# Keeping the tiled matmul pieces together by priority instead of by fences, with two score blocks in one bank

## The chip, the cores and the metric

The kernel runs on one core of a Trainium2 chip. The core has five engines that run their own instruction queues side by side: TensorE (PE, the matmuls; PEld is its weight load), VectorE (DVE), ScalarE (ACT), GpSimd (POOL) and SyncE (SP, which only issues DMA transfers here). Each engine takes its instructions strictly in the order in which they were put into its queue; semaphores make one engine wait for another. The metric is the time of one execution in microseconds (us), measured on the device; lower is better.

## The reference

The program is a causal attention with a decay, followed by a gated MLP. Cut to what matters:

```python
# q, k, v: 8 batches x 8 heads x 576 tokens x 64;  f: 8 x 8 x 576
scores = q @ k.T / 8
decay  = cumsum(log f)[:, None] - cumsum(log f)[None, :]
scores = where(causal, -1e9, scores + decay)
attn   = exp(scores - max) / (sum + 1e-9)
x      = concat_heads(attn @ v)                 # 8 x 576 x 512
h = relu(x @ w_in); u, v = halves of h          # 512 columns each
v_n = (v - mean) / sqrt(var + 1e-6)
v_s = w_spatial @ v_n + b_spatial               # over the 576 tokens
out = (u * v_s) @ w_out
```

## The kernel before

**Work units.** Attention goes by pairs of heads: 32 pairs P, four to a batch. One pair's two heads (h = 0, 1) lie in the two halves of the 128 partitions: head 0 in rows 0 to 63, head 1 in rows 64 to 127. The MLP ("moe" in the code) goes by batches, eight of them. The outer loop at the end of the kernel writes attention of batch b+1 and the MLP of batch b interleaved, at a pace set by the numbers that the generators yield. The order so written is the priority order; the tile framework's scheduler then decides, for each engine, in which order the instructions really stand in its queue. It may take a later instruction first when an earlier one is not yet ready in its own timeline.

**Attention of one pair.** `scores(P)` makes, for each of the first four 128-row blocks i of queries and each head, one matmul of 64 contraction rows (L257): block i sees 128·(i+1) keys, so its output has 128, 256, 384 or 512 columns. The output tile is `sc` (PSUM pool `s`, four banks). `lowest` (L243, DVE) adds the decay `dk` and writes the result into `tt`, one tile for each head, `tt0` and `tt1`, which exist once only; ACT takes the exponential in place (L267); DVE makes the reciprocal sums `sm` (L270, L271); POOL multiplies each block by them (L275). `transposes(P, h)` turns the blocks of `tt` with TensorE (L321, into `tp`, PSUM pool `t`, two banks), and the results are copied into `e` by ACT and DVE in turn (L313). The last 64 queries of both heads are done together in `scores_tail` (matmul at L201 into `sc`, then tile `tl`) and `transposes_tail` (L332). `attend` (L350) multiplies `e` with the raw V: 14 matmuls into two `sc` tiles, x0 (queries 0 to 255) and x1 (the rest); the two heads write the two halves of the output partitions. `prep(P)` loads `qk_t` (two buffers), `dk` and `dt` (one buffer each) through SP and masks `dk` and `dt` on POOL (L216, L218, L222).

**Tiled pieces.** The matmuls of `scores` use 64 of the array's 128 rows each, those of `attend` 64 of its 128 columns, so those of head 0 and head 1 can run at the same time when they stand next to each other. The kernel calls such a group a piece. There are three pieces for each pair: score blocks 0 and 1, score blocks 2 and 3, and `attend`. `in_one_piece` and `queued` put fences around them: every matmul and transpose that is written before a piece must stand in TensorE's queue before it, everything written after it must stand behind it, and the matmuls inside it are chained one behind the other.

**MLP of one batch.** First the v half: five groups of matmuls into `ps` (PSUM pool `ps_m`, two banks) and the normalization (L424 to L437). Then the u half (L448), then for two token ranges the spatial product (L466 to L471), the gate `u` (L474, DVE), its split into `gh` (L477, ACT) and `gl` (L478, POOL), and `w_out_tile` (L494), two at a time, which multiplies four `gh`/`gl` pairs j = 0 to 3 with `w_out`. The matmuls that use `gl` of j = 3 cannot start before POOL has made it.

**Startup.** At the start weights are loaded and split into high and low parts by DVE, ACT and POOL (`load64`, L114 to L128), beside the attention of batch 0 alone.

## Time and profile before

| | |
|---|---|
| runs of the kernel before | 878.43, 881.36, 887.39 us (median 881.36) |
| the profiled execution's own time | 876.43 us |
| its span, first to last instruction | 874.7 us |
| granted TensorE clock, mean | 0.965 |
| DVE busy, share of the span | 444.2 us, 51% |
| ACT busy | 415.0 us, 47% |
| POOL busy | 383.5 us, 44% |

The profile is one execution. A row with "busy" gives the time in which an engine had at least one instruction under way. Idle time before an instruction is put down to the engine whose semaphore came last. Matmuls overlap in the array, so the duration of one is longer than the distance from its start to the next one's start; the distance between starts is what a matmul costs in a full stream.

### The profile page before, as it was taken

What the parts mean: (1) busy time and instruction counts of PE and PEld (TensorE: products, weight loads), DVE (VectorE), ACT (ScalarE), POOL (GpSimd) and SP (SyncE); (2) the same over time, 40 slices, a digit from 0 to 9 for tenths busy, and PEclk for the clock granted to TensorE, in tenths of its full rate; (3) what the DMA queues carried; (4) which work ended last, traced back from release to release, by engine and by line L of the source; (5) the groups of instructions that cost most, each with busy time, mean ns of one, the idle gap of its engine ahead of it and who ended that gap; (6) DMA issues with size and microseconds to landing.
All of it is one profiled execution on the core that took longest, in us unless ns stands there. A gap on an engine that the chain in (4) does not pass through costs nothing.

```text
span 874.7 us, 14557 instructions
## 1 busy us (share of the span) xinstructions
PE 789.7 (90%) x4933; PEld 610.6 (70%) x4934; DVE 444.2 (51%) x1482; ACT 415.0 (47%) x1092; POOL 383.5 (44%) x703
## 2 busy tenths in 40 slices
PE   5677889988998989988999889989899889999997
PEld 2344557876687867866688767867678766787896
DVE  6865856334654537445564336445463345643131
ACT  3565655434554435544564336544554345643231
POOL 4875675443544236334453336343354434432141
PEclk8677889999999999999999999999999999999999
DMA  6545531233232233233321243322322333101001
GB/s 232 169 140 144 164 95 64 85 112 112 88 88 73 67 97 88 88 112 85 99 73 62 83 123 89 88 85 64 102 65 85 112 106 90 50 26 40 25 1 61
DMA packets 35213, 79.44 MB, mean 91 GB/s; under 512 B 4161, under 2 KB 8257, under 8 KB 35138
## 3 DMA queue, kind: packets, MB, share of 16 engines
q1 hardware_dynamic: 34818, 77.98, 29.7%
q8 instruction: 39, 0.64, 0.3%
q10 hardware_dynamic: 320, 0.52, 0.2%
q14 instruction: 36, 0.29, 0.1%
HBM read 68.73 MB, written 9.75 MB: 90 GB/s over the span
## 4 chain that ended last, share of the span: by engine, by line
PE 52%; POOL 16%; ACT 7%; issue 6%; DVE 3%; DMA 3%; POOLq 0%; SPq 0%; ACTq 0%; DVEq 0%
PE ps L201 29%; PE sc L350 7%; POOL tt L275 7%; PE sc L257 5%; PE tp L321 5%; PE sc L201 3%; POOL vnl L433 3%; ACT tt L267 3%; DMA dt<-rows_d 3%; PE tp L201 2%; POOL gl L478 2%; ACT e L313 2%; POOL dk L218 1%; POOL dk L216 1%; PE tp L332 1%
## 5 line engine op out<-in xcount | busy, mean ns | idle before, releaser
L275 POOL TENSOR_SCALAR tt<-tt,sm 128x128 f32<-128x128 f32 (+3 forms) x256 | 134.6, 545 | 149.3 <-DVE sm L271 121.4
L267 ACT ACTIVATE tt<-tt,nm 128x128 f32<-128x128 f32 (+3 forms) x256 | 141.3, 554 | 56.2 <-DVE nm L243 55.5
L321 PE MATMUL tp<-ident,tt 128*128 128x128 f32 x640 | 104.5, 290 | 35.6 <-ACT e L313 20.4
L478 POOL TENSOR_TENSOR gl<-u,gh 128x256 fp32r<-128x256 f32 (+1 forms) x64 | 51.5, 804 | 178.5 <-ACT gh L477 178.4
L321 PEld LDWEIGHTS tp<-ident,tt 128*128 128x128 f32 x640 | 77.4, 146 | 55.6 <-ACT e L313 25.6
L313 DVE COPY e<-tp 128x128 f32<-128x128 f32 (+2 forms) x160 | 66.9, 420 | 90.0 <-PE tp L321 73.6
L257 PE MATMUL sc<-qk_t 64*128 64x384 f32 (+3 forms) x512 | 97.4, 492 | 9.6 <-DVE nm L243 9.6
L313 ACT COPY e<-tp 128x256 f32<-128x256 f32 (+2 forms) x160 | 75.6, 478 | 61.6 <-PE tp L321 49.8
L350 PE MATMUL sc<-e,vraw 128*64 128x320 f32 (+4 forms) x896 | 96.1, 365 | 2.7 <-DVE nm L243 1.6
L350 PEld LDWEIGHTS sc<-e,vraw 128*64 128x64 f32 x896 | 60.2, 139 | 43.0 <-issue 4.5
L201 PE MATMUL ps<-xh,winh 128*128 128x256 f32 (+1 forms) x232 | 74.5, 321 | 0.5 <-ACT vx L424 0.5
L201 PE MATMUL ps<-sph,vnh 128*128 128x256 f32 (+1 forms) x240 | 74.7, 311 | 0.0
L201 PE MATMUL ps<-woh,gl 128*128 128x512 f32 x112 | 45.3, 406 | 29.2 <-POOL gl L478 29.2
L201 PE MATMUL ps<-spl,vnh 128*128 128x256 f32 (+1 forms) x240 | 71.5, 298 | 0.0
L201 PE MATMUL ps<-sph,vnl 128*128 128x256 f32 (+1 forms) x240 | 71.4, 297 | 0.0
L201 PE MATMUL ps<-xl,winh 128*128 128x256 f32 (+1 forms) x232 | 68.5, 295 | 0.0
L201 PE MATMUL ps<-xh,winl 128*128 128x256 f32 (+1 forms) x232 | 68.5, 295 | 0.0
L257 PEld LDWEIGHTS sc<-qk_t 64*128 64x128 f32 x512 | 44.6, 202 | 34.0 <-DVE nm L243 16.8
L356 DVE TENSOR_TENSOR xl<-sc,xh 128x256 fp32r<-128x256 f32 x64 | 29.1, 454 | 75.7 <-ACT xh L355 75.5
L243 DVE CUSTOM_DVE_ANT_1 tt<-sc,dk 128x512 f32<-128x512 f32 (+1 forms) x128 | 66.5, 553 | 1.0 <-PE sc L257 0.9
L243 DVE CUSTOM_DVE_ANT_0 tt<-sc,dk 128x384 f32<-128x384 f32 (+1 forms) x128 | 49.4, 421 | 34.6 <-PE sc L257 32.4
L201 PE MATMUL ps<-winh,xh 128*128 128x512 f32 x148 | 63.4, 429 | 0.0
(165 smaller groups left out, 1680.3 us busy)
## 6 DMA issues: line engine op xcount, KB each, us to landing
dk<-rows_d SPq DMA_DIRECT2D x64, 320.0 KB, 4.0
qk_t<-in_dram SPq DMA_DIRECT2D x32, 608.0 KB, 4.6
vraw<-in_dram SPq DMA_DIRECT2D x32, 320.0 KB, 2.9
dt<-rows_d SPq DMA_DIRECT2D x64, 144.0 KB, 4.4
out_dram<-o SPq DMA_DIRECT2D x32, 256.0 KB, 2.0
w<-in_dram SPq DMA_DIRECT2D x8, 512.0 KB, 5.0
w<-in_dram SPq DMA_DIRECT2D x8, 256.0 KB, 3.3
wraw<-in_dram SPq DMA_DIRECT2D x4, 288.0 KB, 7.3
```

Source lines behind the costliest of these rows:

```text
L201: queued(T.matmul(o, l, r, start=st, stop=sp))
L216: G.affine_select(out=two, in_=two, compare_op=ALU.is_ge, fill=-8.0 * BIG, base=0, pattern=[[0, 2], [-1, 128]], channel_multiplier=1)
L243: V.tensor_tensor_reduce(out=out, in0=ps, in1=dec, scale=-0.125, scalar=3.0e38, op0=ALU.add, op1=ALU.min, accum_out=acc_)
L257: made.append(T.matmul(sc[i, h][:, 0:n], qk_t[p, n - 128:n], qk_t[p, 640:640 + n], start=True, stop=True))
L267: last["exp", P, h, i] = A.activation(t, t, AF.Exp, bias=nm[h][:, i:i + 1], scale=-1.0, accum_out=sm[h][:, i:i + 1])
L275: G.tensor_scalar(out=t, in0=t, scalar1=sm[h][:, i:i + 1], scalar2=1.0, op0=ALU.mult, op1=ALU.mult)
L313: (V.tensor_copy if nev[0] % 2 == 1 else A.copy)(out, ps)
L321: queued(T.transpose(out=tp[:, (i - c) * 128:(i - c + 1) * 128], in_=tt[h][:, TOFF[i] + 128 * c:TOFF[i] + 128 * c + 128], identity=ident))
L350: made.append(T.matmul(x[64 * h:64 * h + 64, q0 - s0:q1 - s0], vt[:, c, h, :], e[:, h, e0 + q0:e0 + q1], start=c == 0, stop=c == end))
L356: V.tensor_tensor(out=xl[:, s0:s0 + n], in0=ps[:, 0:n], in1=f32(xh[:, s0:s0 + n]), op=ALU.subtract)
L433: G.tensor_tensor(out=tlo, in0=x, in1=f32(th[:]), op=ALU.subtract)
L478: G.tensor_tensor(out=gl[j][:, 0:nt], in0=g, in1=f32(gh[j][:, 0:nt]), op=ALU.subtract)
```

## The change

Three things change.

1. The fences go. Plain matmuls and transposes are issued without any edge. A piece is now given as a list of jobs: its first matmul is issued like any other instruction; each further one is issued at the highest priority, with an edge that puts it behind the one before it in TensorE's queue. Nothing keeps other matmuls out from between two matmuls of a piece when the second one is not ready in the scheduler's timeline.
2. The two score pieces are cut in another way: blocks 0, 1 and 2 in one, block 3 alone in the other, and within a piece from the largest block down. Blocks 0 and 1 of a head share a bank (columns 0 to 127 and 128 to 383), so the first piece needs four `sc` tiles, as before, and the second two where it needed four. The pace numbers are unchanged as formulas.
3. `transposes_tail` does blocks 4 and 3 before 0, 1 and 2, and `attend` lists x1 before x0.

```diff
-    def queued(i):
-        if fence:
-            behind(i, fence[0])
-        open_.append(i)
-        return i
-
-    def in_one_piece(made):
-        for n, i in enumerate(made):
-            for j in open_ if n == 0 else (made[n - 1],):
-                behind(i, j)
-        open_.clear()
-        fence[:] = [made[-1]]
+    def in_one_piece(jobs):
+        was = None
+        for n, job in enumerate(jobs):
+            if was is None:
+                was = job()
+            else:
+                with tc.high_priority():
+                    i = job()
+                behind(i, was)
+                was = i
 
     def mm(o, l, r, st, sp):
-        queued(T.matmul(o, l, r, start=st, stop=sp))
+        T.matmul(o, l, r, start=st, stop=sp)
...
-        for piece in ((0, 1), (2, 3)):
-            made, sc = [], {}
+        for piece in ((0, 1, 2), (3,)):
+            at = {}
             for i in piece:
                 for h in range(2):
-                    sc[i, h] = PS['s'].tile([128, 512], F32, name="sc")
-                    p, n = slice(64 * h, 64 * h + 64), 128 * (i + 1)
-                    made.append(T.matmul(sc[i, h][:, 0:n], qk_t[p, n - 128:n], qk_t[p, 640:640 + n],
-                                         start=True, stop=True))
-            in_one_piece(made)
+                    if i == 1:
+                        at[i, h] = at[0, h][0], 128
+                    else:
+                        at[i, h] = PS['s'].tile([128, 512], F32, name="sc"), 0
+
+            def product(i, h):
+                ps, c = at[i, h]
+                p, n = slice(64 * h, 64 * h + 64), 128 * (i + 1)
+                return lambda: T.matmul(ps[:, c:c + n], qk_t[p, n - 128:n], qk_t[p, 640:640 + n],
+                                        start=True, stop=True)
+
+            in_one_piece([product(i, h) for i in reversed(piece) for h in range(2)])
...
-        for cs, off, step in (((0, 1, 2), 512, 512), ((4, 3), 576, 640)):
+        for cs, off, step in (((4, 3), 576, 640), ((0, 1, 2), 512, 512)):
...
-            for x, s0, q0, q1, end in ((x0, 0, 128 * c, 256, 1), (x1, 256, lo, S, NB)):
-                for h in range(2) if c <= end else ():
-                    made.append(T.matmul(x[64 * h:64 * h + 64, q0 - s0:q1 - s0], vt[:, c, h, :],
-                                         e[:, h, e0 + q0:e0 + q1], start=c == 0, stop=c == end))
-        in_one_piece(made)
+            for x, s0, q0, q1, end in ((x1, 256, max(256, 128 * c), S, NB), (x0, 0, 128 * c, 256, 1)):
+                jobs += [product(x, s0, q0, q1, c, h, end) for h in range(2) if c <= end]
+        in_one_piece(jobs)
```

The softmax rows after a score piece follow the new order of blocks (largest first within a piece). In the new code `lowest` stands at L238, the score matmuls at L258, plain matmuls at L196, the transposes at L325 and L336, `attend` at L352, the POOL scaling at L279 and `gl` at L484.

What this does to the queues is shown at three places. First TensorE, at the scores of the tenth pair (P = 9), beside the v half of an MLP. In the names `sc` are score banks, `ps` the MLP's banks, `tp` the transposes' banks, `tt_82` and `tt_83` the tiles of head 0 and head 1. Before:

```order
L321 MATMUL tp<-ident,tt_82 128x128 x3
L321 MATMUL tp<-ident,tt_83 128x128 x10
L257 MATMUL sc<-qk_t 128x128 x2
L257 MATMUL sc<-qk_t 128x256 x2
L201 MATMUL ps<-winh,xh 128x512
L201 MATMUL ps<-winl,xh 128x512
L201 MATMUL ps<-winh,xl 128x512
L201 MATMUL ps<-winh,xh 128x512
L201 MATMUL ps<-winl,xh 128x512
L201 MATMUL ps<-winh,xl 128x512
L257 MATMUL sc<-qk_t 128x384 x2
L257 MATMUL sc<-qk_t 128x512 x2
```

Both pieces stand whole, behind all transposes of the pair before. Now, the first piece at the same pair:

```order
L258 MATMUL sc<-qk_t 128x384 x2
L258 MATMUL sc<-qk_t 128x256
L196 MATMUL ps<-winh,xl 128x512
L196 MATMUL ps<-winh,xh 128x512
L196 MATMUL ps<-winl,xh 128x512
L258 MATMUL sc<-qk_t 128x256
L258 MATMUL sc<-qk_t 128x128 x2
L325 MATMUL tp<-ident,tt_82 128x128
L325 MATMUL tp<-ident,tt_83 128x128 x4
```

The piece is cut between the 256-column matmul of head 0 and that of head 1, and it stands ahead of the last transpose of head 0 and all of head 1. Now, the second piece at this pair:

```order
L258 MATMUL sc<-qk_t 128x512
L196 MATMUL ps<-winh,xh 128x512
L196 MATMUL ps<-winl,xh 128x512
L196 MATMUL ps<-winh,xl 128x512
L196 MATMUL ps<-winh,xh 128x512
L196 MATMUL ps<-winl,xh 128x512
L258 MATMUL sc<-qk_t 128x512
L325 MATMUL tp<-ident,tt_83 128x128 x5
```

Five MLP matmuls stand between the two heads' 512-column matmuls. Over the whole program TensorE's queue has 92 unbroken runs of tiled matmuls before and 127 now. For the pairs P = 5 to 31, which lie where TensorE is nearly always busy, 14 pieces are cut between the 256-column matmuls of the two heads, 11 between the 512-column ones, and 5 more between two blocks (behind both 384-column matmuls); three times a score piece now joins directly to an `attend`.

Second POOL, at the last gate product of a `w_out` group (j = 3, the row with `gl`) while the scores of P = 8 are scaled (`tt0`, `tt1`) and the next pair's `dk` is masked. Before:

```order
L275 TENSOR_SCALAR tt0_82<-tt0_82,sm_2119 128x256
L275 TENSOR_SCALAR tt0_82<-tt0_82,sm_2119 128x384
L275 TENSOR_SCALAR tt0_82<-tt0_82,sm_2119 128x512
L216 AFFINE_SELECT dk_2268<-dk_2268 128x2x128
L218 AFFINE_SELECT dk_2268<-dk_2268 128x256
L275 TENSOR_SCALAR tt1_83<-tt1_83,sm_2120 128x128
L275 TENSOR_SCALAR tt1_83<-tt1_83,sm_2120 128x256
L275 TENSOR_SCALAR tt1_83<-tt1_83,sm_2120 128x384
L275 TENSOR_SCALAR tt1_83<-tt1_83,sm_2120 128x512
L216 AFFINE_SELECT dk_2269<-dk_2269 128x2x128
L218 AFFINE_SELECT dk_2269<-dk_2269 128x256
L478 TENSOR_TENSOR gl_2158<-u_1597,gh_2157 128x320
```

Now:

```order
L484 TENSOR_TENSOR gl_2045<-u_1467,gh_2044 128x320
L484 TENSOR_TENSOR gl_2089<-u_1530,gh_2088 128x320
L279 TENSOR_SCALAR tt0_82<-tt0_82,sm_2103 128x128
L279 TENSOR_SCALAR tt0_82<-tt0_82,sm_2103 128x256
L279 TENSOR_SCALAR tt0_82<-tt0_82,sm_2103 128x384
L279 TENSOR_SCALAR tt0_82<-tt0_82,sm_2103 128x512
L211 AFFINE_SELECT dk_2250<-dk_2250 128x2x128
L213 AFFINE_SELECT dk_2250<-dk_2250 128x256
L484 TENSOR_TENSOR gl_2128<-u_1583,gh_2127 128x320
L279 TENSOR_SCALAR tt1_83<-tt1_83,sm_2104 128x128
L279 TENSOR_SCALAR tt1_83<-tt1_83,sm_2104 128x256
L279 TENSOR_SCALAR tt1_83<-tt1_83,sm_2104 128x384
```

The last `gl` of the group stands ahead of head 1's four scalings and two masks instead of behind them. This holds at all such groups in which a pair's scaling falls between the third and the fourth `gl`.

Third TensorE in the startup, at the scores of P = 2 and the transposes of P = 1. Before (the rows ahead are P = 1's other transposes):

```order
L321 MATMUL tp_526<-ident_63,tt1_83 128x128
L321 MATMUL tp_545<-ident_63,tt1_83 128x128
L321 MATMUL tp_550<-ident_63,tt1_83 128x128
L321 MATMUL tp_554<-ident_63,tt1_83 128x128
L257 MATMUL sc_561<-qk_t_480 128x128
L257 MATMUL sc_563<-qk_t_480 128x128
L257 MATMUL sc_565<-qk_t_480 128x256
L257 MATMUL sc_567<-qk_t_480 128x256
L257 MATMUL sc_577<-qk_t_480 128x384
L257 MATMUL sc_579<-qk_t_480 128x384
L257 MATMUL sc_581<-qk_t_480 128x512
L257 MATMUL sc_583<-qk_t_480 128x512
```

Now:

```order
L258 MATMUL sc_559<-qk_t_476 128x384
L258 MATMUL sc_560<-qk_t_476 128x384
L325 MATMUL tp_503<-ident_63,tt0_82 128x128 x2
L325 MATMUL tp_510<-ident_63,tt0_82 128x128
L325 MATMUL tp_503<-ident_63,tt0_82 128x128
L325 MATMUL tp_510<-ident_63,tt0_82 128x128
L325 MATMUL tp_515<-ident_63,tt0_82 128x128
L325 MATMUL tp_503<-ident_63,tt0_82 128x128
L325 MATMUL tp_510<-ident_63,tt0_82 128x128
L325 MATMUL tp_515<-ident_63,tt0_82 128x128
L325 MATMUL tp_519<-ident_63,tt0_82 128x128
L258 MATMUL sc_557<-qk_t_476 128x256
```

The scores of the next pair no longer stand behind the last transpose of this pair: blocks 2 stand ahead of head 0's transposes, the rest between those of head 0 and head 1. On SP the load of the sixth of the eight `w_in` chunks, which stood between the two `dk` loads of P = 1, now stands behind both of them, the `qk_t` load of P = 2 and the two `dt` loads of P = 1.

More of the change, by code (lines that the diff above doesn't have):

```diff
@@ L177, in attn_gmlp_kernel @@
     G.memset(f32(vb_[64:66, :]), 1.0)
-    open_, fence = [], []
     def behind(i, j):
@@ L262, in scores @@
             yield 250 + 1.68 * 128 * sum(i + 1 for i in piece)
-            for (i, h), ps in sc.items():
-                n = 128 * (i + 1)
-                t = tt[h][:, TOFF[i]:TOFF[i] + n]
-                lowest(t, ps[:, 0:n], decay(dk[h], i), nm[h][:, i:i + 1])
-                last["exp", P, h, i] = A.activation(t, t, AF.Exp, bias=nm[h][:, i:i + 1], scale=-1.0,
-                                                    accum_out=sm[h][:, i:i + 1])
+            for i in reversed(piece):
+                for h in range(2):
+                    ps, c = at[i, h]
+                    n = 128 * (i + 1)
+                    t = tt[h][:, TOFF[i]:TOFF[i] + n]
+                    lowest(t, ps[:, c:c + n], decay(dk[h], i), nm[h][:, i:i + 1])
+                    last["exp", P, h, i] = A.activation(t, t, AF.Exp, bias=nm[h][:, i:i + 1], scale=-1.0,
+                                                        accum_out=sm[h][:, i:i + 1])
         for h in range(2):
@@ L320, in transposes @@
             for i in range(c, NB):
-                queued(T.transpose(out=tp[:, (i - c) * 128:(i - c + 1) * 128],
-                                   in_=tt[h][:, TOFF[i] + 128 * c:TOFF[i] + 128 * c + 128], identity=ident))
+                T.transpose(out=tp[:, (i - c) * 128:(i - c + 1) * 128],
+                                   in_=tt[h][:, TOFF[i] + 128 * c:TOFF[i] + 128 * c + 128], identity=ident)
             e0 = EOFF[c]
@@ L331, in transposes_tail @@
             for j, c in enumerate(cs):
-                queued(T.transpose(out=tp[:, j * 128:(j + 1) * 128], in_=tl[:, c * 128:(c + 1) * 128],
-                                   identity=ident))
+                T.transpose(out=tp[:, j * 128:(j + 1) * 128], in_=tl[:, c * 128:(c + 1) * 128],
+                            identity=ident)
             pv = tp[:, 0:128 * n].rearrange("p (c h s) -> p c h s", h=2, s=64)
@@ L343, in attend, with product @@
         x0, x1 = (PS['s'].tile([128, 512], F32, name="sc") for _ in range(2))
-        made = []
-        for c in range(NB + 1):
-            e0 = EOFF[c] - 128 * c
-            lo = max(256, 128 * c)
-            for x, s0, q0, q1, end in ((x0, 0, 128 * c, 256, 1), (x1, 256, lo, S, NB)):
-                for h in range(2) if c <= end else ():
-                    made.append(T.matmul(x[64 * h:64 * h + 64, q0 - s0:q1 - s0], vt[:, c, h, :],
-                                         e[:, h, e0 + q0:e0 + q1], start=c == 0, stop=c == end))
-        in_one_piece(made)
+        jobs = []
+        def product(x, s0, q0, q1, c, h, end):
+            e0 = EOFF[c] - 128 * c
+            return lambda: T.matmul(x[64 * h:64 * h + 64, q0 - s0:q1 - s0], vt[:, c, h, :],
+                                    e[:, h, e0 + q0:e0 + q1], start=c == 0, stop=c == end)
+        for c in range(NB + 1):
+            for x, s0, q0, q1, end in ((x1, 256, max(256, 128 * c), S, NB), (x0, 0, 128 * c, 256, 1)):
+                jobs += [product(x, s0, q0, q1, c, h, end) for h in range(2) if c <= end]
+        in_one_piece(jobs)
         yield 2950
```

## The prediction

> **What bounds the kernel now.** I read the page first, then the busy time by stage, then who made TensorE (PE) wait in each stage, then the timelines around these waits. The page:
>
> ```profile
> span 874.7 us, 14557 instructions
> PE 789.7 (90%) x4933; PEld 610.6 (70%) x4934; DVE 444.2 (51%) x1482; ACT 415.0 (47%) x1092; POOL 383.5 (44%) x703
> ```
>
> PE is busy for nine tenths of the span and no other engine comes near. The busy times by stage, one row for the startup, one for the long middle, one for the last MLP:
>
> ```profile
> 0.00:140.00 140.00, 104.53 (x502) 62.32 (x503) 96.81 (x300) 73.44 (x192) 93.00 (x152) 0.80 0.53 157
> 140.00:802.00 662.00, 618.38 (x4031) 489.28 (x4031) 328.74 (x1136) 322.85 (x861) 273.46 (x528) 1.00 0.28 84
> 802.00:874.70 72.70, 66.75 (x404) 58.96 (x403) 18.63 (x48) 18.69 (x39) 17.03 (x24) 0.98 0.08 26
> ```
>
> Columns: length, then busy time of PE, PEld, DVE, ACT, POOL, the granted clock, the DMA share and rate. In the middle PE is idle for 662.0 − 618.4 = 43.6 us at full clock; in the startup for 140.0 − 104.5 = 35.5 us at a granted clock of 0.80. The last stage has no attention in it and is not touched. So the change can win at most the idle time, and what it adds to PE's own work in the middle is paid in full. PE's waits in the middle (waited for; us in total, times, longest), then those of the startup that are over 2 us:
>
> ```profile
> PE ps L201 <- POOL gl L478: 29.2, 13, 2.6
> PE tp L321 <- ACT e L313: 11.5, 32, 0.4
> PE tp L321 <- DVE e L313: 2.0, 7, 0.3
> ...
> PE tp L321 <- POOL tt L275: 10.2, 3, 5.2
> PE sc L257 <- DVE nm L243: 9.6, 3, 7.3
> PE tp L321 <- ACT e L313: 8.6, 4, 4.3
> ```
>
> Two kinds make up the middle: 13 waits of 2.2 us for the last `gl` of a `w_out` group, and 39 of 0.35 us in which a transpose waits for a bank that ACT or DVE has yet to empty. The pieces themselves wait for nothing there.
>
> **The change part by part.**
>
> *The cut pieces (a loss).* What does a run of tiled matmuls cost? Both score pieces of one pair in the middle, with the plain matmuls around them (columns: start, duration, engine, line, what, count of instructions):
>
> ```profile
> 371.93 0.93 PE L257 MATMUL sc<-qk_t 64*128 64x128 f32 x8
> 372.79 0.39 PE L201 MATMUL ps<-sph,vnh 128*128 128x256 f32 x1
> 373.01 0.28 PE L201 MATMUL ps<-spl,vnh 128*128 128x256 f32 x1
> ...
> 374.07 0.28 PE L201 MATMUL ps<-sph,vnl 128*128 128x256 f32 x1
> 374.28 1.77 PE L257 MATMUL sc<-qk_t 64*128 64x384 f32 x8
> 375.99 0.38 PE L201 MATMUL ps<-sph,vnh 128*128 128x256 f32 x1
> 376.21 0.28 PE L201 MATMUL ps<-spl,vnh 128*128 128x256 f32 x1
> 376.33 0.28 PE L201 MATMUL ps<-sph,vnl 128*128 128x256 f32 x1
> ```
>
> From start to start the first piece (128 + 256 columns for each head) takes 372.79 − 371.93 = 0.86 us, the second (384 + 512) 375.99 − 374.28 = 1.71 us. The 512 columns more cost 0.85 us, 1.66 ns for a column of both heads. Then 384 columns are 0.64 us, and 0.22 us of the first piece are fixed. Outside, the plain matmul ahead of a piece takes 0.21 us instead of 0.12 (374.07 to 374.28 against 376.21 to 376.33), the one behind it 0.22 (375.99 to 376.21): 0.19 us more. A run costs 0.41 us beside its columns. That the two heads run side by side shows in the sums of the middle:
>
> ```profile
> L257 PE MATMUL sc<-qk_t 64*128 64x512 f32 x104 | 26.6, 589 | 0.0
> L257 PE MATMUL sc<-qk_t 64*128 64x384 f32 x104 | 23.8, 535 | 0.0
> ```
>
> 104 instructions of 589 ns would be 61 us one by one; the engine is busy for 26.6. So a head whose partner is cut off streams alone: between nothing (were the heads not side by side) and the whole 0.85 us at 512 columns, 0.42 at 256. I take the whole, since the overlap is as good as full. In the middle the order of the queue has 14 + 11 + 5 cuts and 3 joins with `attend`: (30 − 3) × 0.41 = 11.1 us of runs, 14 × 0.42 = 5.9 us and 11 × 0.85 = 9.4 us of lone heads. Sum +26.4 us; ends 11 (heads not side by side) and 26.4. Startup cuts fall into idle time and are set to nothing there; without that cover they would be 8 × 0.41, 3 us. Pieces left whole cost the same: blocks 0, 1, 2 and block 3 are two runs with the same columns as before. [...]
>
> *The `gl` waits (a gain).* One of them on PE, and POOL's queue in the same stretch:
>
> ```profile
> 382.01 0.40 PE L201 MATMUL ps<-woh,gh 128*128 128x512 f32 x1
> 382.25 0.40 PE L201 MATMUL ps<-wol,gh 128*128 128x512 f32 x1
> 384.86 0.50 PE L201 MATMUL ps<-woh,gl 128*128 128x512 f32 x1 [2.22 <-POOL gl L478]
> ```
>
> ```profile
> 378.56 2.06 POOL L275 TENSOR_SCALAR tt<-tt,sm 128x128 f32<-128x128 f32 x4 [2.62 <-DVE sm L271]
> 380.58 0.41 POOL L216 TENSOR_SCALAR_AFFINE_SELECT dk<-dk 128x256 f32<-128x256 f32 x1
> 380.94 0.41 POOL L218 TENSOR_SCALAR_AFFINE_SELECT dk<-dk 128x256 f32<-128x256 f32 x1
> 381.33 2.06 POOL L275 TENSOR_SCALAR tt<-tt,sm 128x128 f32<-128x128 f32 x4
> 383.35 0.41 POOL L216 TENSOR_SCALAR_AFFINE_SELECT dk<-dk 128x256 f32<-128x256 f32 x1
> 383.71 0.41 POOL L218 TENSOR_SCALAR_AFFINE_SELECT dk<-dk 128x256 f32<-128x256 f32 x1
> 384.08 0.72 POOL L478 TENSOR_TENSOR gl<-u,gh 128x256 fp32r<-128x256 f32 x1
> ```
>
> `gl` stands behind the scalings and masks of both heads. In the new order it stands behind head 0's alone, so it moves from 384.08 to 381.33: 2.75 us earlier, more than the 2.22 us of wait. PE also comes later, since tail transposes and the next pair's first transposes now stand between the matmuls on `gh` and on `gl`. What is late next is head 1's scaling, by the 0.72 us of `gl`; its transposes stand several MLP groups behind. I leave 5 of the 29.2 us, for the pairs whose block 3 is cut and so comes late: gain 24. Ends: 29, and 12 (below).
>
> *The transpose waits (a gain).* Before, all ten transposes of a head stand in a row ahead of the fence, on two banks; each 0.35 us wait is a copy not yet done. Now MLP matmuls stand between most groups of transposes of different banks, two or more at 0.23 us each (382.01 to 382.25), which covers 0.35. I take 9 of the 13.5 us; ends 0 and 13.5.
>
> *New waits in the pieces (a loss).* The second score piece now needs banks that DVE has read a moment ago, and `attend` follows the tail's transposes closely. Before, such waits are nothing in the middle (no row of that kind among the waits above), and in the startup 9.6 us in three. In the order the distance from piece to piece is some 5 us of PE work, and from the last tail transpose to `attend` mostly 1.8 us; a copy is under half a us (the rows of DVE and ACT at 379.86 and 379.64 below). I take 3 us; ends 0 and 27 pairs × 1.2 us = 32: a wait of 0.91 as at 84.14 below, and a third more.
>
> *The startup (a gain).* One round of it on PE, with the first MLP matmul; the two copies spoken of; and two rows of POOL:
>
> ```profile
> 76.78 0.48 PE L321 MATMUL tp<-ident,tt 128*128 128x128 f32 x2 [4.32 <-ACT e L313]
> 78.18 1.97 PE L321 MATMUL tp<-ident,tt 128*128 128x128 f32 x8 [0.93 <-DVE e L313]
> 80.08 3.15 PE L257 MATMUL sc<-qk_t 64*128 64x128 f32 x12
> 84.14 3.08 PE L257 MATMUL sc<-qk_t 64*128 64x512 f32 x4 [0.91 <-DVE nm L243]
> ...
> 108.85 0.50 PE L201 MATMUL ps<-winh,xh 128*128 128x512 f32 x1
> ```
>
> ```profile
> 379.86 0.42 DVE L313 COPY e<-tp 128x256 f32<-128x256 f32 x1 [0.89 <-PE tp L332]
> 379.64 0.48 ACT L313 COPY e<-tp 128x384 f32<-128x384 f32 x1 [1.08 <-PE tp L332]
> ```
>
> ```profile
> 73.12 2.06 POOL L275 TENSOR_SCALAR tt<-tt,sm 128x128 f32<-128x128 f32 x4
> 92.12 2.45 POOL L275 TENSOR_SCALAR tt<-tt,sm 128x128 f32<-128x128 f32 x4 [1.35 <-DVE sm L271]
> ```
>
> The round is a chain: scaling (73.12), transposes (to 80.08), scores (80.08 to some 87.2), DVE, ACT, scaling (92.12), 19 us. DVE cannot write `tt` before the transposes have read it. In the new order the scores of blocks 0 to 2 are already in their banks by then, and head 0 goes on while head 1 is still turned. The first 3.15 us of the scores leave the chain, in four rounds, since pairs 1 to 4 are scored before the MLP begins at 108.85: 12.6 us. DVE is busy for 97 and POOL for 93 of the 140 us, with weights that have to be done anyway, so I take 9. Ends: 21, the three startup waits of the transposes, all but nothing left; and a loss of 5, one wait like the longest (5.2 us), should a score piece stand ahead of transposes with its banks or `qk_t` not there. SP's moved load of a `w_in` chunk feeds the u half, which the MLP takes up after its whole v half; it comes later and costs nothing.
>
> *Order inside.* x1 before x0, blocks 4 and 3 first, larger blocks first: the same instructions, zero; `attend` now starts on the columns that the last copy of the tail fills, which is in the new waits.
>
> Sum: +26.4 − 24 − 9 + 3 − 9 = −12.6, so −13 us. Against the profiled execution, 876.4 us (span 874.7 and 1.7 around it), that is 863.4. The runs' median is 881.4, 0.6% above the profiled one; on that scale I forecast 868.
>
> **The rivals.**
>
> *More is won.* The startup chain gives 20 us instead of 9 and all transpose waits go (4.5 more): −13 − 15.5 is −28.5, 853. For it: POOL and DVE idle in the startup in long stretches. Against: the weights' work there stays.
>
> *The gain goes elsewhere.* `gl` now stands right behind a mask of `dk`, which must wait for its load. If the loads land late, POOL stands still and half of the `gl` waits stay: −13 + 12 = −1, 880. Against: in the row at 380.58 the mask follows the scaling without a wait.
>
> *Slower.* The other side by one mechanism: PE takes its queue in order, and the matmuls at highest priority stand at the first place where the scheduler's own clock had their bank free. If DVE is later on the chip, everything behind waits. The price is bounded above by 1.2 us for each of 27 pairs, 32 us; with 32 instead of 3 the sum is −13 + 29 = +16, 897, and with a startup that wins nothing +25, 906. It decides at 0.6 us a pair (13 + 3 = 16 us in 27 pairs) against no change, at 0.9 us against 1% slower. Against: DVE is busy half of the time, and the distances above.
>
> *It does nothing.* Excluded: 127 runs instead of 92 are another program.
>
> **How the numbers follow.** About 1% (8.8 us: below 872.6, above 890.2) is what a measurement of this kernel can tell from no change. Chances: the forecast 0.56 (its own range 858 to 880; 0.40 of it faster, 0.16 same), more won 0.16 (faster), the gain elsewhere 0.15 (same), slower 0.13. So faster 0.56, same 0.31, slower 0.13. The range of 8 in 10 goes from 850, with the lower half of "more won" left out (0.08), to 892, with most of "slower" left out (0.11).
>
> **What would show it.** Right: the wait of plain matmuls for `gl` below 8 us in all; transposes' waits below 6; score instructions in several short groups, with PE busy time in the middle some 20 us or more above 618; the MLP's first matmul well before 108.9 us. Wrong: waits of score matmuls for DVE of more than 15 us, a `gl` wait of 15 or more, or a startup as long as before. A PE busy sum that does not rise would mean that cut pieces cost less than I think.

## The result and the profile after

The changed kernel takes 827.3 us in the median of 4 runs (823.34 to 830.39). The kernel before, timed beside it, takes 879.89 us (872.94 to 887.39). The ratio is 0.9425, with a 95% interval of 0.9338 to 0.9511: faster by more than the 868 us that were forecast, and by more than the range down to 850 allows.

The profiled execution of the changed kernel took 830.26 us, 46.2 us less than the 876.43 of before. The page of the changed kernel, with its span and its busy times:

```profile
span 828.5 us, 14548 instructions
PE 802.9 (97%) x4934; PEld 620.8 (75%) x4934; DVE 441.5 (53%) x1482; ACT 408.2 (49%) x1092; POOL 387.2 (47%) x703
```

PE works 13.2 us longer than before (802.9 against 789.7), to which more cut pieces add (0.54 us for each run in e1, below), and is idle for 25.6 us instead of 85.0. So the gain is idle time, and some of it is given back as work. The same by stage (length, then busy time of PE, PEld, DVE, ACT and POOL, granted clock, DMA share and rate):

```profile
0.00:140.00 140.00, 120.14 (x582) 75.05 (x583) 108.48 (x314) 77.47 (x203) 99.55 (x157) 0.83 0.51 157
140.00:765.00 625.00, 625.00 (x4000) 494.45 (x3999) 316.61 (x1129) 314.23 (x857) 272.49 (x524) 1.00 0.28 89
765.00:828.50 63.50, 57.71 (x356) 51.34 (x354) 16.41 (x40) 16.49 (x34) 15.21 (x22) 0.98 0.09 30
```

In the middle PE has no idle time left at all. Both kinds of wait that made up the 43.6 us of before are gone, the one for `gl` and the one of the transposes for a bank. These are the longest of the waits that the changed kernel still has (waited for; us in total, times, longest); all four kinds lie in the first 140 us:

```profile
PE sc L258 <- DVE nm L238: 6.3, 3, 2.8
PE sc L196 <- DVE nm L238: 4.0, 3, 1.7
PE ps L196 <- ACT vx L430: 2.6, 1, 2.6
PE sc L352 <- DVE e L317: 2.6, 3, 1.3
```

The MLP's first matmul, on PE's timeline, starts 8.7 us earlier than the 108.85 of before:

```profile
100.11 0.50 PE L196 MATMUL ps<-winh,xh 128*128 128x512 f32 x1
```

Since durations of matmuls overlap (in the prediction's row at 382.01 one lasts 0.40 us, and the next starts 0.24 us after its start), I add up the distances from each matmul's start to the next one's, from the trace's records. From the MLP's first matmul to the end they sum to 760.2 us before and 722.2 after:

| from start to start, us | before | after | e5 (below) |
|---|---|---|---|
| until the MLP's first matmul | 108.9 | 100.1 | 103.1 |
| plain matmuls of the MLP | 486.8 | 462.3 | 453.1 |
| transposes of the heads | 89.5 | 57.0 | 55.3 |
| score pieces | 69.9 | 90.3 | 69.1 |
| attend | 81.6 | 80.0 | 80.1 |
| tails (scores and transposes) | 32.4 | 32.7 | 41.6 |

The plain matmuls lose 24.5 us and the transposes 32.5; the score pieces take 20.4 back. The transposes are the surprise: the profile of before lists only 19.0 us of idle time in these 89.5.

### The profile page after: what moved, and what is told of

It reads as the page before. It is cut to its first block, busy times and chain, and to the rows that moved or that the text cites. A ratio compares the mean times of both kernels' runs of the same rounds, so it can differ in the third digit from the quotient of the medians.

```text
span 828.5 us, 14548 instructions
## 1 busy us (share of the span) xinstructions
PE 802.9 (97%) x4934; PEld 620.8 (75%) x4934; DVE 441.5 (53%) x1482; ACT 408.2 (49%) x1092; POOL 387.2 (47%) x703
## 4 chain that ended last, share of the span: by engine, by line
PE 85%; POOL 1%; issue 0%; DVE 0%; ACT 0%; POOLq 0%
PE ps L196 47%; PE sc L258 11%; PE sc L352 10%; PE tp L325 8%; PE sc L196 5%; PE tp L196 2%; PE tp L336 2%; POOL tt L279 0%; POOL vnl L439 0%; POOL mv L434 0%; POOL w L126 0%; POOL wol L128 0%; ACT o L508 0%; ACT vx L430 0%; DVE st L431 0%
## 5 line engine op out<-in xcount | busy, mean ns | idle before, releaser
L279 POOL TENSOR_SCALAR tt<-tt,sm 128x128 f32<-128x128 f32 (+3 forms) x256 | 134.8, 545 | 154.5 <-DVE sm L275 110.0
L271 ACT ACTIVATE tt<-tt,nm 128x384 f32<-128x384 f32 (+3 forms) x256 | 142.6, 558 | 99.1 <-DVE nm L238 86.6
L258 PE MATMUL sc<-qk_t 64*128 64x128 f32 (+3 forms) x512 | 123.3, 481 | 6.6 <-DVE nm L238 6.3
L325 PE MATMUL tp<-ident,tt 128*128 128x128 f32 x640 | 113.0, 287 | 2.4 <-POOL tt L279 2.4
L317 DVE COPY e<-tp 128x384 f32<-128x384 f32 (+1 forms) x160 | 71.0, 447 | 70.8 <-PE tp L325 56.0
L317 ACT COPY e<-tp 128x256 f32<-128x256 f32 (+1 forms) x160 | 71.4, 450 | 71.8 <-PE tp L325 45.5
L325 PEld LDWEIGHTS tp<-ident,tt 128*128 128x128 f32 x640 | 78.9, 145 | 36.6 <-POOL tt L279 6.7
L484 POOL TENSOR_TENSOR gl<-u,gh 128x256 fp32r<-128x256 f32 (+1 forms) x64 | 51.3, 802 | 107.3 <-ACT gh L483 107.1
L352 PE MATMUL sc<-e,vraw 128*64 128x320 f32 (+4 forms) x896 | 95.4, 365 | 2.6 <-DVE e L317 2.6
L352 PEld LDWEIGHTS sc<-e,vraw 128*64 128x64 f32 x896 | 60.1, 138 | 40.9 <-DVE e L317 4.8
L238 DVE CUSTOM_DVE_ANT_1 tt<-sc,dk 128x256 f32<-128x256 f32 (+1 forms) x128 | 70.3, 552 | 36.6 <-PE sc L258 22.3
L258 PEld LDWEIGHTS sc<-qk_t 64*128 64x128 f32 x512 | 55.0, 191 | 38.8 <-issue 15.2
L196 PE MATMUL ps<-xh,winh 128*128 128x256 f32 (+1 forms) x232 | 74.0, 319 | 2.6 <-ACT vx L430 2.6
L196 PE MATMUL ps<-sph,vnh 128*128 128x256 f32 (+1 forms) x240 | 76.4, 318 | 0.0
L196 PE MATMUL ps<-spl,vnh 128*128 128x256 f32 (+1 forms) x240 | 71.8, 299 | 0.0
L196 PE MATMUL ps<-sph,vnl 128*128 128x256 f32 (+1 forms) x240 | 71.4, 297 | 0.0
L196 PE MATMUL ps<-xl,winh 128*128 128x256 f32 (+1 forms) x232 | 70.7, 305 | 0.0
L196 PE MATMUL ps<-xh,winl 128*128 128x256 f32 (+1 forms) x232 | 70.2, 303 | 0.0
L238 DVE CUSTOM_DVE_ANT_0 tt<-sc,dk 128x128 f32<-128x128 f32 (+1 forms) x128 | 53.4, 419 | 22.5 <-PE sc L258 12.9
L196 PE MATMUL ps<-winh,xh 128*128 128x512 f32 x148 | 61.5, 416 | 0.0
L196 PE MATMUL ps<-winl,xh 128*128 128x512 f32 x148 | 59.5, 402 | 0.0
L483 ACT CAST gh<-u 128x256 fp32r<-128x256 f32 (+1 forms) x64 | 27.6, 433 | 58.1 <-DVE u L480 41.5
```

The costliest lines, as they stand in the source:

```text
L196: T.matmul(o, l, r, start=st, stop=sp)
L238: V.tensor_tensor_reduce(out=out, in0=ps, in1=dec, scale=-0.125, scalar=3.0e38, op0=ALU.add, op1=ALU.min, accum_out=acc_)
L258: return lambda: T.matmul(ps[:, c:c + n], qk_t[p, n - 128:n], qk_t[p, 640:640 + n], start=True, stop=True)
L271: last["exp", P, h, i] = A.activation(t, t, AF.Exp, bias=nm[h][:, i:i + 1], scale=-1.0, accum_out=sm[h][:, i:i + 1])
L279: G.tensor_scalar(out=t, in0=t, scalar1=sm[h][:, i:i + 1], scalar2=1.0, op0=ALU.mult, op1=ALU.mult)
L317: (V.tensor_copy if nev[0] % 2 == 1 else A.copy)(out, ps)
```

## The experiments

The ratio given with each is to the kernel before on the same chip. "Runs" are unbroken runs of tiled matmuls in TensorE's queue: 92 before, 127 after. The edits are shown cut to their core; those of e1, e2, e2b, e5 and e6 are against the changed kernel, that of e11 is against e5, the others are against the kernel before.

**e1 and e2: each half of the change alone.** e1 has the new `in_one_piece` and no fences, but the old division, a bank for each block and the old orders:

```diff
-        for piece in ((0, 1, 2), (3,)):
+        for piece in ((0, 1), (2, 3)):
...
-                    if i == 1:
-                        at[i, h] = at[0, h][0], 128
-                    else:
-                        at[i, h] = PS['s'].tile([128, 512], F32, name="sc"), 0
+                    at[i, h] = PS['s'].tile([128, 512], F32, name="sc"), 0
```

> The changed kernel with the old division of the scores ((0,1) and (2,3), a bank for each block) and the old orders: only the fences are replaced by the edge and the priority. The order has 227 unbroken runs of tiled matmuls here, 127 in the changed kernel and 92 before. Theory (removing the fences saves some 66 us: 32 for the waits for gl, 26 for the transposes' waits, 9 in the startup; each extra run costs 0.55 us, which is 20 us over 35): 100 runs more than the changed kernel, 827 + 55 = 882 us. By the prediction's own price of 0.75 us per cut: 902. Rival (a cut costs nothing, the gain is the fences alone): 827.

Measured: 887.64 us, ratio 1.0159 (1.0109 to 1.0209). PE in e1, from its page:

```profile
PE 857.0 (97%) x4934; PEld 616.1 (70%) x4934; DVE 448.7 (51%) x1482; ACT 416.6 (47%) x1092; POOL 386.9 (44%) x703
```

PE is idle for 28.6 us of 885.6, about as little as after the whole change, so the waits are gone here too. But 100 more runs make 54.1 us more busy time than in the changed kernel, 0.54 us for each. A cut is not free, and the fences' removal alone is slower than before.

e2 is the other half: fences as before, with the new division, the shared bank and the new orders.

```diff
-        was = None
-        for n, job in enumerate(jobs):
...
+        made = [job() for job in jobs]
+        for n, i in enumerate(made):
+            for j in open_ if n == 0 else (made[n - 1],):
+                behind(i, j)
```

> The fences of the kernel before are kept; the new division ((0,1,2) and (3), blocks 0 and 1 in one bank), and the new orders of blocks, of the tails and of attend. 92 runs of tiled matmuls, as before. Theory (the gain is the removal of the fences): 880 us, within 1% of before. Rival (the gain comes from the shared bank and the earlier release of banks): 835 to 855.

Measured: 918.58 us, ratio 1.0515 (1.0463 to 1.0566). Neither the theory nor the rival had it. e2b tells the division from the orders: as e2, but the tails' transposes and attend's two halves in the old order.

```diff
-        for cs, off, step in (((4, 3), 576, 640), ((0, 1, 2), 512, 512)):
+        for cs, off, step in (((0, 1, 2), 512, 512), ((4, 3), 576, 640)):
...
-            for x, s0, q0, q1, end in ((x1, 256, max(256, 128 * c), S, NB), (x0, 0, 128 * c, 256, 1)):
+            for x, s0, q0, q1, end in ((x0, 0, 128 * c, 256, 1), (x1, 256, max(256, 128 * c), S, NB)):
```

> As e2 (fences, new division, blocks 0 and 1 in one bank, larger blocks first), but the tails' transposes and the two halves of attend in the old order. In e2 the matmuls of attend took 96.8 us from start to start instead of 77.3, and the waits for gl 50.0 instead of 29.5. Theory (the order inside attend makes PE stand within the piece for the last copy of the tail, 19 us; the division makes the waits for gl longer, 20 us): 918 - 19 = 899 us. Rival (all of it is the division): 918. Rival (all of it is the order of tail and attend): 880.

Measured: 913.03 us, ratio 1.0439 (1.0344 to 1.0534). The difference of some 5 us from e2 is not clear of the two intervals, so the orders matter little if at all; it is the division (with the shared bank and the larger blocks first) that hurts while the fences stand. One of e2's waits, first on POOL and then on PE (start, duration, engine, line, what, and in brackets the idle time ahead of it and who ended it):

```profile
389.34 2.06 POOL L285 TENSOR_SCALAR tt<-tt,sm 128x128 f32<-128x128 f32 x4 [1.70 <-DVE sm L281]
...
392.43 2.06 POOL L285 TENSOR_SCALAR tt<-tt,sm 128x128 f32<-128x128 f32 x4
...
395.19 0.75 POOL L304 TENSOR_SCALAR tl<-tl,sm 128x576 f32<-128x576 f32 x1
395.90 0.73 POOL L490 TENSOR_TENSOR gl<-u,gh 128x256 fp32r<-128x256 f32 x1
```

```profile
392.05 0.40 PE L202 MATMUL ps<-wol,gh 128*128 128x512 f32 x1
396.68 0.80 PE L202 MATMUL ps<-woh,gl 128*128 128x512 f32 x1 [4.24 <-POOL gl L490]
397.41 3.35 PE L358 MATMUL sc<-e,vraw 128*64 128x320 f32 x18
```

`gl` now stands behind the scalings of both heads and of the tail, so PE waits 4.24 us where it waited 2.2 to 2.6. Of the 2.02 us more than the wait of 2.22 in the prediction's rows, 0.75 is the tail's scaling and 0.29 a wait of POOL for a load of `dk` (at 391.69, not shown above); for the rest, POOL begins this scaling 1 us later against PE's queue. And more follows: the next 18 matmuls of attend take 3.35 us, while in the kernel before all 28 took 2.92. The busy times around it show why (columns as above, the clock third from the end):

```profile
392.00:396.70 4.70, 0.47 (x3) 0.03 (x2) 0.00 (x0) 0.00 (x0) 4.70 (x11) 0.96 0.64 206
396.70:400.10 3.40, 3.40 (x13) 1.65 (x15) 0.00 (x0) 0.59 (x1) 0.35 (x2) 0.55 0.20 77
400.10:408.00 7.90, 7.90 (x61) 7.25 (x58) 2.58 (x8) 2.33 (x5) 0.88 (x1) 1.00 0.24 75
```

After the wait the granted clock is halved for 3.4 us. In the trace's clock records between 130 and 820 us, e2 has 13 such stretches with 54.6 us in all, the profiled execution of before has one with 3.4 us, and the changed kernel has none. Half of the 51.2 us more is up to 25.6 us lost; some 5 us of PE's idle time lie inside these stretches, so it is nearer 23. With 20.7 us more of waits for `gl` (50.0 against 29.2 in all) and 7.4 less in the startup, that makes 36 to 39 of the 41.0 us by which e2's span is longer.

**g0, g3, g4, e4: which fence costs what.** To free one kind of instruction without cutting pieces, the first matmul of a piece here waits for all that the later ones need: the readers of the banks that the piece will write, and for attend the copies into `e`.

```diff
+    def in_one_piece(made, needs):
+
+        for i in needs:
+            tc.add_manual_dep(made[0].ins, i.ins.name, mybir.DependencyInfo(
+                mybir.DependencyClass.Sync, mybir.DependencyReason.DATA), reason="whole")
...
```

g0 is the kernel before with this alone.

> The kernel before with all its fences; only the first matmul of each piece waits for all that the later ones of the piece need, as in g3 and g4 (92 runs, as before). Theory (this wait alone does nothing, the gains of g3 and g4 are those of the fences): 880 us, within 1% of before. Rival (the wait keeps PE from standing inside a piece and is itself a part of the gain of g3 and g4): 850 to 865.

Measured: 885.95 us, ratio 1.0063 (1.0010 to 1.0116). The wait by itself wins nothing. g3 adds that transposes stand outside the fences, g4 that plain matmuls do:

```diff
-                queued(T.transpose(out=tp[:, (i - c) * 128:(i - c + 1) * 128],
+                (T.transpose(out=tp[:, (i - c) * 128:(i - c + 1) * 128],
```

```diff
-        queued(T.matmul(o, l, r, start=st, stop=sp))
+        T.matmul(o, l, r, start=st, stop=sp)
```

> The kernel before, fences kept for the plain matmuls, but the transposes stand outside them; the first matmul of each piece waits for all that the later ones of the piece need, so that pieces are seldom cut (105 runs instead of 92). Theory (each transpose that waited for its bank cost 0.51 us, 25.7 us in all; 13 runs more at 0.55 us are +7): 880 - 19 = 861 us. Rival (the 13.5 us of idle time listed for the transposes are their whole price): 880 - 14 + 7 = 873. Rival (transposes alone can't help, since nothing else fills PE there): 887.

> The kernel before, fences kept for the transposes, but the plain matmuls of the MLP and of the tail's scores stand outside them; the first matmul of each piece waits for all that the later ones need (92 runs as before, none more). Theory (waits for gl 32 us and the startup's 9 go, the transposes' waits stay): 880 - 41 = 839 us. Rival (free plain matmuls fill the transposes' waits too): 880 - 41 - 26 = 813. Rival (gl's waits need the transposes free as well, since these stand between gh and gl): 871.

Measured: g3 843.61 us, ratio 0.9663 (0.9604 to 0.9723), better than all three values expected for it; g4 814.86 us, ratio 0.9323 (0.9278 to 0.9367). The waits of g3 after the MLP's first matmul, the two longest kinds:

```profile
PE tp L337 <- ACT e L329: 7.2, 16, 1.3
PE ps L216 <- POOL gl L497: 5.3, 7, 0.9
```

In g3 most of the waiting for `gl` is gone (5.3 us against 29.2), since transposes now fill it, but transposes still wait for their banks; that they have little else than themselves to stand behind is argued, not shown. In g4 there is next to nothing left, on the whole way from the MLP's first matmul to the end:

```profile
PE ps L216 <- ACT vx L443: 1.8, 1, 1.8
PE sc L273 <- DVE nm L258: 1.1, 1, 1.1
PE tp L337 <- ACT e L329: 0.4, 1, 0.4
```

These three are all, and none is for `gl`. Free plain matmuls fill both kinds of wait. That was the rival in my expectation, 813 us, and it is what freeing the plain matmuls alone is worth.

e4 is g4 without the added wait, so that pieces are cut.

> As g4 (plain matmuls outside the fences, transposes inside them), but the first matmul of a piece waits for nothing extra: 136 runs instead of 92. Theory (0.54 us for each run): 815 + 24 = 839 us. Rival (a cut costs less where the work between is needed anyway): 815 to 825.

Measured: 826.91 us, ratio 0.9421 (0.9351 to 0.9491). The expectation counts 136 runs, but the program that ran has 127, in its queue and in its trace: 12 us for 35 runs, 0.34 each by the medians and 0.25 by the ratios. Of the 35 added cuts, all behind the MLP's first matmul, 28 lie in attend between its x0 and x1 halves, where the two heads stay side by side; only 7 separate the heads of a 512 column block. From start to start the 28 cost attend 4.2 us (80.0 in g4, 84.2 in e4), 0.15 each, and the 7 cost the score pieces 7.7 (69.7 and 77.4), 1.1 each. Here a cut's price depends on what it parts.

**e5, e10, e6, e11: the changed kernel with fewer or more runs.** e5 adds the wait of g0 to the changed kernel (96 runs); e10 has the old division besides (94), with blocks 0 and 1 still in one bank and the new orders.

```diff
-    def in_one_piece(jobs):
+    def in_one_piece(jobs, needs):
...
                 was = job()
+                for i in needs:
+                    tc.add_manual_dep(was.ins, i.ins.name, mybir.DependencyInfo(
+                        mybir.DependencyClass.Sync, mybir.DependencyReason.DATA), reason="whole")
...
```

> The changed kernel, and the first matmul of each piece waits for all that its later ones need (the readers of the banks, the evacuations), so that nothing is put between: 96 runs instead of 127. Theory (0.54 us for each run, as e1 against the changed kernel has it: PE's busy time 857.0 - 802.9 over 100 runs): 827 - 17 = 810 us. Rival (the pieces now wait as long as the cuts cost, since what was put between was work): 827.

> As e5, with the scores divided (0,1) and (2,3) as before, blocks 0 and 1 still in one bank: 94 runs. Theory (once pieces are whole and no fence stands, the division is worth nothing): as e5, 810 us, within 1% of it. Rival (three blocks ahead is worth something by itself, since DVE gets its work in larger lots): 820 or more.

Measured: e5 814.32 us, ratio 0.9265 (0.9191 to 0.9339); e10 817.45 us, ratio 0.9311 (0.9242 to 0.9380). e5 is faster than both kernels of this case. The score matmuls' own busy time on PE, from the MLP's first matmul to the end, in before, after and e5 (length, then busy time of PE and PEld, clock, DMA share and rate):

```profile
108.90:874.70 765.80, 73.71 (x432) 33.22 (x432) 0.99 0.27 80
```

```profile
100.10:828.50 728.40, 96.11 (x432) 43.78 (x432) 1.00 0.26 83
```

```profile
103.10:807.80 704.70, 72.84 (x432) 37.17 (x432) 1.00 0.28 87
```

The same 432 matmuls need 22.4 us more after the change, and e5, whose pieces are whole, gives all of that back. In the medians e5 is 13 us faster than the changed kernel, in the two profiled executions 20.7; these two lie at opposite ends of their runs, so 0.4 to 0.7 us for each of 31 runs is as close as this comes. e10 is within 1% of e5: with whole pieces and no fences the division is worth nothing that can be told.

e6 drops the priority and keeps the edges (170 runs):

```diff
-                with tc.high_priority():
-                    i = job()
+                i = job()
```

> The changed kernel with the edges but without the highest priority: 170 runs of tiled matmuls in the order instead of 127. Theory (the priority does nothing but keep pieces together; 43 runs at 0.42 us, from e5 against the changed kernel, up to 0.75, the prediction's price): 827 + 18 to 32 = 845 to 859 us. Rival (an added run costs 0.27, as e4 against g4): 839. Rival (edges alone bring the whole gain, cuts or not): 827.

Measured: 856.50 us, ratio 0.9803 (0.9719 to 0.9886), 29 us more than the changed kernel, inside the 18 to 32 expected. In the new rule the priority is what holds pieces together.

e11 goes below 92 runs: block 3's score matmuls join attend's piece (65 runs).

```diff
-        in_one_piece(jobs, made_e[-10:] + freed(2))
+        in_one_piece(first + jobs, made_e[-10:] + freed(4 if first else 2))
...
+        if rest:
+            rest()
```

> As e5, but the score matmuls of block 3 are taken out of their own piece and put ahead of attend's in one piece: 65 runs instead of 96. Its lowest, exponentials and the scaling of that pair come after attend. Theory (a run costs 0.41 us beside its columns, the fixed part that the prediction read from one pair): 814 - 13 = 801 us. Rival (the softmax of block 3 comes later by half a pair, its transposes wait, and these waits eat the gain): 814 or more.

Measured: 843.71 us, ratio 0.9644 (0.9567 to 0.9722). The rival had it. A joined piece needs all four banks at once and stands still for them, on PE at 399.85:

```profile
397.82 0.55 PE L374 MATMUL tp<-ident,tl 128*128 128x128 f32 x3 [0.24 <-DVE e L355]
399.85 1.83 PE L277 MATMUL sc<-qk_t 64*128 64x512 f32 x4 [1.49 <-DVE nm L253]
401.61 3.87 PE L393 MATMUL sc<-e,vraw 128*64 128x320 f32 x28
```

From the MLP's first matmul on, all waits of PE listed in e11 sum to 24.1 us against 4.9 in e5, and the clock records have five stretches of 3.41 us at half clock there before the last 5 us, up to 8.5 us lost, where e5 has none: some 28 of the 33.8 us between the two profiled executions.

**d1 and d2: what a wait costs.** The kernel before, with one (d1) or two (d2) more subtractions on POOL ahead of the last `gl` of a group:

```diff
+                for _ in range(2 if j == NJ - 1 else 0):
+                    more = G.tensor_tensor(out=spare[:, 0:128], in0=g[:, 0:128], in1=f32(gh[j][:, 0:128]), op=ALU.subtract)
...
```

> The kernel before, with one more subtraction of 128 columns on POOL (into a tile that nobody reads) ahead of the last gl of each w_out group; by the forms of 256 and 320 columns (732 and 877 ns) it takes some 0.44 us. The 12 waits of 2.2 to 2.6 us in the middle become 2.7 to 3.1. Theory (a wait costs its length, and from some length between 2.8 us, the longest after which the clock stayed whole, and 3.7 us, the shortest after which it was always halved, a stretch of 3.4 to 6.8 us at half clock besides): most of these waits are still short, 880 + 5 = 885 us, up to 910 where all are followed by such a stretch. Rival (a wait costs its length alone): 885.

> The same with two such subtractions; the scaling of the tail (764 ns) now also stands ahead of gl, so that the waits become 3.9 to 4.3 us. Theory (each is followed by a stretch of half clock; in e2 13 of them held 54.6 us, 27.3 us lost): 880 + 12 x 1.64 + 12 x 2.1 = 925 us. Rival (a wait costs its length alone): 900.

Measured: d1 886.18 us, ratio 1.0149 (1.0088 to 1.0210); d2 912.41 us, ratio 1.0451 (1.0393 to 1.0509). The wait for `gl` between 140 and 820 us, in d1 and in d2:

```profile
PE ps L202 <- POOL gl L485: 34.5, 13, 3.0
```

```profile
PE ps L202 <- POOL gl L485: 47.0, 12, 4.1
```

By the clock records 3 of d1's 12 waits over 2.6 us are followed by a half clock stretch (10.2 us in all) and all 12 of d2's (44.4 us). Theory and rival both put d1 at about 885 us, so it does not part them; d2 does. For d2 against before: 47.0 us of long waits instead of 28.5 is 18.5 more, and half of 41.0 us more at half clock is 20.5; together 39, where the profiled execution is 36.0 us longer. The rival, which charges a wait its length alone, gave 900 us and falls; the theory's 925 is somewhat high. So e2's loss is, but for some 2 to 5 us, its longer waits for `gl` and the clock behind them; the new division has no larger price besides.

## Why the prediction was wrong

The mechanism was right: the `gl` waits and the transposes' waits go, the startup gets shorter, cut pieces give something back, and the score pieces wait for nothing in the middle. Of the signs that it named for being right one did not come: from the MLP's first matmul on PE's busy time rose by 7.9 us (712.1 to 720.0), not by 20 in the middle. Of the signs for being wrong none came. What failed is the size of its terms, and all but the startup erred the same way: the transposes' waits by 16.7 us, the `gl` waits and the cut pieces by some 7 each, the new waits by 3. On the profiled executions:

| term | forecast, us | measured, us | from |
|---|---|---|---|
| transposes' waits | -9 | -25.7 | starts, below |
| waits for `gl` | -24 | -31.3 | 29.2 listed from the MLP's first matmul on, and 13 x 0.16 |
| cut pieces | +26.4 | +19.0 | what remains of -38.0 |
| new waits in the pieces | +3 | 0 | no row in the middle |
| startup | -9 | -8.7 | 108.85 to 100.11 |
| sum | -12.6 | -46.7 | |

*The transposes' waits: the step that failed.* The prediction said "I take 9 of the 13.5 us; ends 0 and 13.5". 13.5 was no end. Three rows of before on PE show it, a transpose that stands alone and a group of ten:

```profile
166.79 0.27 PE L321 MATMUL tp<-ident,tt 128*128 128x128 f32 x1
...
168.66 0.93 PE L321 MATMUL tp<-ident,tt 128*128 128x128 f32 x7
169.94 0.63 PE L321 MATMUL tp<-ident,tt 128*128 128x128 f32 x3 [0.35 <-ACT e L313]
```

One transpose lasts 0.27 us, seven last 0.93, so in a stream they start 0.11 us apart. Without a wait the eighth would start at 168.66 + 7 x 0.11 = 169.43. It starts at 169.94, 0.51 us later. The profile lists 0.35, because it counts idle time from the end of the seventh (169.59), and that end lies 0.16 us behind the moment at which the next could have started. The records of before have 41 such distances of about 0.62 us instead of 0.11, 21.0 us lost, and three longer ones with 4.7: 25.7 us. The changed kernel has none. Of the 25.7 us, 19.9 lie in the middle that the prediction's term covers, on the 39 waits listed with 13.5; the other 5.8 lie at 114 to 119 us and at 805, where no term of it looked. And they all went: I took two thirds of the listed time, since I asked which groups of transposes have two plain matmuls between them; on the chip no transpose in the middle waits at all.

The rest of the 32.5 us in the table of starts is for the most part a shift between its rows: a transpose of the heads with a plain matmul behind it has the next start after 0.03 us (median) instead of 0.11, and there are 160 such places instead of 64; the plain matmul bears the difference. The same 0.16 us explain the sign that did not come: ahead of 57 waits, 13 for `gl` and 44 of transposes, the busy time of before has 0.16 us each that is really waiting, 9.1 us in all.

*The `gl` waits.* "I leave 5 of the 29.2 us, for the pairs whose block 3 is cut": nothing was left. Here too each wait is 0.16 us longer than listed: in the rows that the prediction shows, plain matmuls start 0.24 us apart, and the one that waits starts 2.61 us after the one ahead, 2.37 late for a listed 2.22, the same 0.15 to 0.16 us.

*The cut pieces.* 26.4 us was the upper end, and I took it. 19.0 is a remainder, and some 2.7 us too low: the half clock stretches behind the MLP's first matmul (10.2 us before, 3.4 after) cost the kernel before up to 4.4 us and the changed one 1.7. e5 measures the cuts without the rest: 722.2 - 699.1 = 23.1 us from start to start with 31 runs fewer. e1 has 0.54 us for each run, e6 29/43 = 0.68. The prediction's price is 0.98 us for each of its 27 runs, so reading fixed cost and lone heads off one pair was somewhat too dear. The cuts are also why the change wins no more: e5 shows what it left lying.

*The new waits.* The "slower" rival, score pieces that wait for DVE in the middle, did not come; there is not one such row. It comes in e11, where a piece needs four banks just after they were read (1.49 us at 399.85 above).

*The startup.* The number is as forecast, -8.7 against -9. e2 has 7.4 of it with all fences standing (first MLP matmul at 101.45). But e1, g3 and e10, all with the old division and free transposes, have 6.4 to 6.9 (102.45, 102.39 and 101.94), and g4, whose transposes stay fenced, has 1.2. So either the new division or free transposes bring most of it, and the two do not add up; which of the prediction's two reasons, scores of blocks 0 to 2 ready sooner or head 0 going on alone, makes it here stays open, and the close number is in part luck.

*The "more is won" rival*, 853 us, had the right direction, but for another reason: 11 of its 15.5 us more were to come from the startup, which gave none of them. For the transposes it too was capped by the listed 13.5 us, so no case reached the time.

What no step of the prediction saw is that the two halves of the change need each other. The fences' removal wins some 60 us only if pieces stay whole: with the old division the new rule cuts so many that it ends 1.6% slower than before. The new division, with the shared bank and the orders, keeps the cuts at 127 runs (which of the three does it was not tested apart), and under fences it makes `gl` later and ends 5% slower. Together they are 5.75% faster. g4 and e5, both at 814 us, show a shorter way to it: free the plain matmuls, and let the first matmul of a piece wait for what the whole piece needs.

## What to carry to other kernels

Price a wait in a stream from the distance between starts, not from the listed idle time, which in before begins 0.16 us too late: its 39 short waits of transposes in the middle were listed with 13.5 us and cost 19.9, half as dear again. Where a group must stay together, let its first instruction wait for everything that the group needs, and let other work flow round it: g4 and e5, made so, take 814.86 and 814.32 us. With the fences PE waited 42.7 us by the list in the middle of before (29.2 for `gl`, 13.5 for the transposes' banks), and the priority alone left 127 runs where e5's wait left 96. And try the halves of a two-part change apart before judging either: here both are slower alone.

## What the runs showed of the hardware

Where TensorE's waits were long, the time grew by more than their length: d2 has 18.5 us more of long waits for `gl` than before (47.0 against 28.5, as listed), and its profiled execution is 36.0 us longer, at a mean granted clock of 0.948 against 0.965. In d2, e2 and e2b (mean granted clock 0.948, 0.942 and 0.951) all 36 waits for `gl` between 140 and 820 us, 3.66 to 4.45 us long, were followed by a granted clock of 0.5, for 3.41 us or twice that in the records. In before and d1 (0.965 both) 4 of 24, 2.2 to 3.0 us long, were followed too, and in the profiled execution of g0 (891.0 us, clock 0.951) 8 of 12, 2.2 to 2.8 us long. A stretch of 3.41 us at half clock costs up to 1.7 us, half its length; that is an estimate.

The shorter waits differ in where they fall. In each of the 15 traces, all changes of the clock lie on a grid of 3.413 us, within 2 ns. These are windows of that grid in before, two around the wait that ends at 384.86 and two around the one that ends at 713.8 (length, then busy time of PE, PEld, DVE, ACT and POOL, granted clock, DMA share and rate):

```profile
380.78:384.20 3.42, 1.86 (x9) 1.17 (x7) 1.18 (x7) 1.28 (x3) 3.42 (x9) 1.00 0.69 226
384.20:387.61 3.41, 2.75 (x22) 1.61 (x24) 0.42 (x1) 0.96 (x2) 1.80 (x4) 1.00 0.43 138
711.88:715.29 3.41, 1.53 (x11) 0.89 (x13) 1.06 (x3) 0.60 (x2) 2.55 (x5) 1.00 0.72 228
715.29:718.70 3.41, 3.41 (x22) 1.99 (x18) 0.42 (x1) 0.37 (x1) 0.47 (x2) 0.50 0.25 82
```

The first wait is split by the border at 384.20, so that no window has more than 1.56 us of idle time, and the clock stays whole. The second leaves 1.88 us idle in one window, and the next window runs at half clock. From 130 us to 5 us before the end, that is the only window of before at full clock that was followed by one at half clock; 214 were followed by another at full clock, and none of them had more than 1.64 us of PE's idle time. The changed kernel has 202 windows there, all at full clock, and PE is idle in none. In all traces together 55 windows at full clock were followed by one at half clock: 54 of them had 1.81 us or more of PE's idle time, one had 1.54. Of the 3051 that were followed by another at full clock, two had more than 1.8 us (1.90 and 1.92). These are counts; no run moves a wait against the grid to test them, and nothing here shows why the clock falls.

The length of a wait alone does not tell the two kinds apart: of the 36 shorter waits in before, d1 and g0 (2.2 to 3.0 us), 12 were followed by half clock and 24 were not. Nor is the grid's place in the kernel the same: its first border lies 1.90 us after the first instruction in before and 0.09 us after it in the changed kernel.
